# One part's distance between the steps of a split, maxima two outputs later, low halves one product later

## The chip, the cores and the metric

The kernel runs on one core of a Trainium2 chip. The metric is device time of one execution in microseconds; the time before is the median of three runs.

## The reference

Attention over 4 x 8 heads of 576 tokens with a threshold on the scores, then two layers without a residual:

```
x = attention(q, k, v, tau)                # 2304 tokens x 512
a, b = x @ w1, x @ w2                      # 2304 x 1024
x2 = ((a * b) @ w3) @ w_out                # 2304 x 512
h = x2 @ w_in                              # 2304 x 2048
g = where(h > 0, h, exp(min(h, 0)) - 1)
out = g @ w_out2                           # 2304 x 512
```

All inputs are float32. The kernel works with pairs of a high and a low half (two float32r or two float16 tensors whose sum is the number), and every product is three matmuls: high with high, high with low, low with high.

## The kernel before

The attention and the products a and b come first, ordered by a planner; that part ends near 510 us and the change does not touch it. From there on each engine's queue is the order of the Python calls, written by hand. SyncE (SP) issues nearly all DMAs, in order, and a DMA that must wait holds those behind it. POOL below is GpSimd.

**The x2 stage.** w3 and w_out were multiplied into M. The tokens are six blocks of 384 (loop `for x, j in enumerate(JS)`), and each block has four outputs of 128 rows (`e`), each of 24 matmuls into one of four PSUM buffers (`ps_x`). A block's g stands as high and low halves in four slots that all six blocks share: while the last output of a block runs, ScalarE makes the high halves of the next block (line 325) and VectorE the low ones (line 326), and then g of the block after that is loaded. For each output `x_size` (line 1200) takes VectorE's maximum from PSUM, and ScalarE copies the output to SBUF (lines 1351 and 1354; from the third block on through `x2s`, two buffers, to DRAM). Two engines do not read one PSUM buffer at the same time here: the second in the order of the calls waits for the first. Beside that, `run_jobs` converts w_in (lines 336 to 350, maximum in line 1265), forms Strassen-like sums of its quarters on POOL (line 1249) and stores seven parts per pair of hidden tiles to DRAM (line 1241).

**The scales.** The halves are float16, so everything is scaled by powers of two from maxima over a whole tensor. `everywhere` sends a maximum per partition to DRAM (line 988) and reads it back to all partitions (line 991); the function that it returns reduces that on VectorE (line 994). There are four such round trips: x2's first pair of blocks (`xg[:, 0:1]`), the weights (`r2`, which gives `w_to`), the other blocks of x2 (`xg[:, 1:3]`), and the output weights (`o_two`, which gives `shift`). The code sends at one place and calls `seen` at a later one.

**The last stage.** For each of three pairs of blocks (`p`) a step goes over one of eight pairs of hidden tiles (`f`), 24 steps. h of a step is a Strassen-like product: seven products of six matmuls (`product`, line 1459, two PSUM buffers), each with its own combination of x2 blocks (`bs[k]`, made by `high_b` on ScalarE and `low_b` on VectorE) and its own part of w_in (`WI[f][:, k]`). The first product is copied by ScalarE (line 1500), the others are added up by VectorE (`sum_of`, line 1485) into four quarters of h. Each quarter then goes through `elu_low`: a minimum (VectorE, line 1397), its exponential (ScalarE, 1398), the maximum that gives g (VectorE, 1401), the high half (ScalarE, 1403) and the low half (VectorE, 1404). After each product, `after(k)` issues five matmuls of the product with w_out2 for the quarters of the step before (`fill`, line 1418, six PSUM buffers `po`); after the last product it issues what is left of them.

In the first pass over f (p = 0) the parts of w_in are still to be split: `load_u` loads part n to a ring of eight buffers `units`, and `split_u` scales it (POOL, line 1300), takes the high half (ScalarE, 1302) and the low half (POOL, 1303), all in one call. `after` makes up to two such calls. The first four steps also convert the last parts of w_out2 (lines 336 to 350, 1021, 1031 to 1033), and at the end of the fifth step the outputs so far, six PSUM buffers, are multiplied by `shift` (lines 1555 and 1557).

Of the kernel before, what the change touches and what calls it, by code (L numbers as in the profile page):

```python
# [10 lines left out]
F16 = mybir.dt.float16  # L11
I32 = mybir.dt.int32
U16 = mybir.dt.uint16
AF = mybir.ActivationFunctionType
ALU = mybir.AluOpType
# [4 lines left out]
P = 128  # L20
# [12 lines left out]
TB = 384  # L33
NB = NT // TB
NPR = NB // 2
NH = NF2 // 2
NC = 7
NUR, NUS = (4, 4), (4, 3)
LEAST_X, LEAST = 2.0 ** -45, 2.0 ** -30
NPL = 4  # L40
WARM = 6
# [227 lines left out]
def attention_moe_moe2(  # L269
# [14 lines left out]
    V, A, G, T, SP = nc.vector, nc.scalar, nc.gpsimd, nc.tensor, nc.sync  # L284
# [10 lines left out]
    W = [None] * 8  # L295
# [518 lines left out]
    for p in range(NPL, NPAIR):  # L814
        t0 = AT[p, 0]
        firsts = [i for i in range(NTILE) if SEQ[i][0] == p]
        for j in range(2):
            h = 2 * p + j
# [259 lines left out]
    def run_jobs(k):  # L1078
        for _ in range(k):
            if jobs:  # L1080
                for fn in jobs.pop(0):
                    fn()
# [116 lines left out]
    def x_size(x, e, o):  # L1199
        V.tensor_reduce(xm[:, 4 * x + e:4 * x + e + 1], o, axis=AX.X, op=ALU.max, apply_absolute_value=True)  # L1200
# [84 lines left out]
    def load_u():  # L1285
        if nu[0] < len(USEQ):
# [2 lines left out]
            SP.dma_start(units[nu[0] % sum(NUR)], wi_dr[f, k])  # L1289
            nu[0] += 1  # L1290

    def split_u():
        n = ns[0]
        if n < len(USEQ):
            f, k = USEQ[n]
            if f not in WI:
                pool, tag = (wp, f"W{4 + f}") if f < 4 else (hop, f"WI{f}")
                WI[f] = pool.tile([P, NC, 2, 2, P], F16, tag=tag, name=f"WI{f}", bufs=1)
            r, t = units[n % sum(NUR)], WI[f][:, k]
            G.tensor_scalar(r, r, w_to, 0.0, op0=ALU.mult, op1=ALU.add)  # L1300
            r = r.rearrange("p (k c) -> p k c", k=2)
            A.activation(t[:, 0], r, AF.Copy)  # L1302
            G.tensor_tensor(t[:, 1], r, t[:, 0], op=ALU.subtract)  # L1303
            ns[0] += 1

    for x, j in enumerate(JS):
        half = x % 2
        for e in range(NK):
# [14 lines left out]
            if x == NB - 1 and e == NK - 1:  # L1323
                for k in (3, 4):
                    high_b(k, 0)
                    low_b(k, 0)
            x_size(x, e, o[:, :TB])
            if x == 2 and e == 0:
                x_sizes(0, xg[:, 0:1])
                seen = everywhere(xg[:, 0:1])  # L1330
            if x == 2 and e == 2:
                seen(xg[:, 0:1])
                x_scale((0,))
            if x == NB - 1 and e == 0:
# [2 lines left out]
                    r2[:, 1:2], cols("wo_two", 8).rearrange("p (a b) -> p a b", a=2)[:, :, :2], axis=AX.XY, op=ALU.max  # L1337
                )
                seen = everywhere(r2)
            if x == NB - 1 and e == 1:  # L1340
                seen(r2)
                power(w_two, r2[:, 0:1], LEAST, 1.0)
                V.tensor_scalar(w_to, w_two, 2.0 ** -11, None, op0=ALU.mult)
                V.reciprocal(w_to, w_to)
                V.tensor_copy(o_two[:, 0:1], r2[:, 1:2])
                h_scale((0,), o_two[:, 0:1])
# [20 lines left out]
            for _ in range(1 + (x * NK + e in (0, 2))):  # L1367
                if len(jobs) > LATE:
                    run_jobs(1)
    run_jobs(len(jobs) - LATE)  # L1370
    ps2.close()
    xw.close()
    mp.close()
# [17 lines left out]
    def elu_low(c):  # L1391

        x, name, dst = c["x"], c["name"], c["dst"]

        def one():
            t = c["t"] = tmp("et", f"et{name}", 2)
            V.tensor_scalar(t, x, 0.0, None, op0=ALU.min)  # L1397
            A.activation(t, t, AF.Exp)  # L1398

        def two():  # L1400
            V.scalar_tensor_tensor(x, c["t"], -1.0, x, op0=ALU.add, op1=ALU.max)  # L1401
            h = hop.tile([P, 2, TB], F16, tag="gg", name=f"gg{name}", bufs=8)
            A.activation(h[:, 0, :], x, AF.Copy, scale=c["by"])  # L1403
            V.scalar_tensor_tensor(h[:, 1, :], x, c["by"], h[:, 0, :], op0=ALU.mult, op1=ALU.subtract)  # L1404
            dst["h"] = h

        return one, two

    def o_mms(p, f, half, dst, first, last):

# [31 lines left out]
            except StopIteration:  # L1442
                oq.pop(0)

    late, highb = [], []
    steps = [(p, f) for p in range(NPR) for f in range(NH)]
    for s, (p, f) in enumerate(steps):
        nm = f"{p}_{f}"
# [4 lines left out]
        def product(k):  # L1453
            w = WI[f][:, k]
            o = ps_h.tile([P, 512], F32, tag="h", name=f"h{nm}_{k}")
            i = 0
            for kt in range(2):
                for wx, xx in ((0, 0), (0, 1), (1, 0)):
                    T.matmul(  # L1459
                        o[:, :TB], w[:, wx, kt, :], bs[k][:, kt, xx, :],  # L1460
                        start=(i == 0), stop=(i == 5),
                    )
                    i += 1
            return o[:, :TB]
# [29 lines left out]
        def plus(n, a, b):  # L1494
            return sum_of(thin[n], a, b)
# [16 lines left out]
        after(0)  # L1512

        u2 = plus(1, product(1), m1)
        after(1)

        quarter("11", product(2), m1)
# [22 lines left out]
        quarter("21", product(5), u3)  # L1540
        lows["22"][1]()
        lows["21"][0]()
        after(5)

        quarter("12", product(6), u4)
        lows["21"][1]()
        lows["12"][0]()
        late.append(lows["12"][1])
        after(6, 99)
        if s == NH // 2:  # L1550
            for h in range(2):
                for t in range(TB // P):
                    o = po[JS[h], t]
                    if t % 2:
                        V.tensor_scalar(o, o, shift, None, op0=ALU.mult)
                    else:
                        A.activation(o, o, AF.Copy, scale=shift)  # L1557
        for q in ("11", "22", "21", "12"):
            oq.append(o_mms(p, f + (NH if q[0] == "2" else 0), int(q[1]) - 1, gg[q], f == 0 and q in ("11", "22"),
                            f == NH - 1 and q in ("21", "12")))  # L1560
        if p + 1 < NPR and f == 1:
            for h in range(2):
                SP.dma_start(bq[:, h], x2_dr[JS[2 * p + 2 + h]])
    while late:
        late.pop(0)()
    fill(999)


# [45 lines left out]
```

## Time and profile before

| | |
|---|---|
| time, median of three runs | 1071.73 us (1071.66 to 1072.56) |
| profiled execution | 1074.29 us, span 1072.5 us |
| granted TensorE clock, mean | 0.969 |
| TensorE busy | 966.8 us (90% of the span) |
| VectorE busy | 771.0 us (72%) |
| ScalarE busy | 556.0 us (52%) |
| GpSimd busy | 437.6 us (41%) |

Times inside the trace count from the start of the span. The granted clock is a share of TensorE's upper level, 2.4 GHz; at the lower one, 1.2 GHz, it is 0.5. Matmuls are pipelined and their ends are modelled, so a TensorE that is shown as busy may still be slow. An idle time in square brackets stands before an instruction, with what ended it.

### The profile page before, as it was taken

The numbers are of one execution on the slowest core, as the hardware profiler recorded it, in microseconds if no ns is written. First come the engines' busy times: TensorE is split into PE (matmuls) and PEld (weight loads), VectorE is DVE, ScalarE is ACT, GpSimd is POOL, SyncE is SP. The second block draws the span as 40 slices with busy tenths as digits, with TensorE's granted clock in tenths as the row PEclk, the third lists the DMA queues.
The fourth block names the chain that finished last, engine by engine and source line by source line (L and its number), as shares of the span: only waits on it lengthen the run. The fifth ranks groups of instructions, "written<-read, shape, count | busy, mean of one in ns | idle before, by whom it ended". The sixth has DMA issues, their size and how long they took to land. (4 is left out here: it accounts for less than half of the span.)

```text
span 1072.5 us, 17102 instructions
## 1 busy us (share of the span) xinstructions
PE 966.8 (90%) x6074; PEld 698.5 (65%) x6074; DVE 771.0 (72%) x1448; ACT 556.0 (52%) x945; POOL 437.6 (41%) x608
## 2 busy tenths in 40 slices
PE   7899999999999999989998876786898999989998
PEld 4456887788889899977897862333344544445553
DVE  6888886888777884979775645665567666766665
ACT  5777776876766763445333424443454333443333
POOL 3468775878788972534210235554340000000000
PEclk9999999999999999999998997988899999999999
DMA  8436765667899787756476564411100200010001
GB/s 250 146 123 157 167 164 133 174 183 182 163 197 192 176 170 221 251 210 241 140 243 213 204 208 124 142 40 47 40 11 29 89 1 1 1 60 1 1 1 60
DMA packets 167282, 138.18 MB, mean 129 GB/s; under 512 B 118332, under 2 KB 153884, under 8 KB 162588
## 3 DMA queue, kind: packets, MB, share of 16 engines
q1 hardware_dynamic: 163084, 107.43, 37.5%
q10 hardware_dynamic: 4112, 29.66, 7.9%
q8 instruction: 48, 0.79, 0.3%
q14 instruction: 38, 0.31, 0.1%
HBM read 84.61 MB, written 24.72 MB: 102 GB/s over the span
## 5 line engine op out<-in xcount | busy, mean ns | idle before, releaser
L1459 PE MATMUL h<-so,WI 128*128 128x384 f16 x1008 | 201.9, 340 | 54.5 <-DVE th L1485 31.4
L681 PE MATMUL ab<-x,W 128*128 128x256 f32 (+1 forms) x1536 | 223.8, 298 | 5.9 <-DVE g L696 4.6
L1418 PE MATMUL o<-WO,gg 128*128 128x512 f16 x864 | 220.7, 390 | 5.8 <-ACT o L1557 4.9
L681 PEld LDWEIGHTS ab<-x,W 128*128 128x128 f32 x1536 | 207.5, 188 | 15.0 <-issue 5.7
L1459 PEld LDWEIGHTS <-WI 128*128 128x128 f16 x1008 | 101.3, 101 | 151.6 <-issue 70.7
L1418 PEld LDWEIGHTS <-gg 128*128 128x128 f16 x864 | 86.3, 100 | 96.3 <-issue 14.4
L526 DVE SCALAR_TENSOR_TENSOR e<-s,st,e 128x576 f32<-128x576 f32 x144 | 115.2, 808 | 23.9 <-ACT e L520 21.8
L1485 DVE SCALAR_TENSOR_TENSOR th<-h,back,th 128x384 f32<-128x384 f32 x168 | 99.0, 611 | 41.5 <-PE h L1459 37.8
L1398 ACT ACTIVATE et<-et 128x384 f32<-128x384 f32 x96 | 50.2, 523 | 143.3 <-DVE et L1397 142.2
L1404 DVE SCALAR_TENSOR_TENSOR gg<-th,c_by,gg 128x384 f16<-128x384 f32 x96 | 60.5, 630 | 87.7 <-ACT gg L1403 87.7
L537 POOL TENSOR_TENSOR hl<-e,hl 128x512 f16<-128x512 f32 x94 | 110.8, 1179 | 25.1 <-ACT hl L533 18.9
L502 DVE TENSOR_REDUCE st<-s 128x1 f32<-128x576 f32 x144 | 105.9, 749 | 18.1 <-PE s L492 10.1
L1313 PE MATMUL x<-sl,M 128*128 128x384 f32 x576 | 107.8, 350 | 10.5 <-DVE sl L326 6.3
L1313 PEld LDWEIGHTS x<-sl,M 128*128 128x128 f32 x576 | 105.2, 198 | 13.0 <-DVE sl L326 8.1
L1403 ACT ACTIVATE gg<-th,c_by 128x384 f16<-128x384 f32 x96 | 58.8, 613 | 71.2 <-DVE th L1401 71.2
L520 ACT ACTIVATE e<-s,st 128x576 f32<-128x576 f32 x108 | 78.4, 736 | 25.6 <-POOL st L510 16.7
L492 PE MATMUL s<-qk 128*128 128x288 f32 x480 | 83.2, 306 | 5.6 <-DVE e L526 4.7
L492 PEld LDWEIGHTS s<-qk 128*128 128x128 f32 x480 | 68.0, 189 | 14.3 <-issue 7.7
L533 ACT ACTIVATE hl<-e 128x576 f16<-128x576 f32 x94 | 63.1, 681 | 22.8 <-DMA pt<-hl 11.2
L1303 POOL TENSOR_TENSOR WI<-wr,WI 128x256 f16<-128x256 f32 x56 | 43.5, 777 | 67.1 <-ACT WI L1302 67.1
L1401 DVE SCALAR_TENSOR_TENSOR th<-et,th 128x384 f32<-128x384 f32 x96 | 54.4, 566 | 17.4 <-ACT et L1398 13.1
L480 PE MATMUL s<-qkp 128*64 128x288 f32 x288 | 43.1, 435 | 7.2 <-ACT pt L578 3.7
(137 smaller groups left out, 1359.2 us busy)
## 6 DMA issues: line engine op xcount, KB each, us to landing
rqk<-in_qk SPq DMA_DIRECT2D x24, 576.0 KB
raw_wo<-in_wo ACTq DMA_DIRECT2D x12, 1024.0 KB
th<-g_dr SPq DMA_DIRECT2D x48, 192.0 KB
raw_w<-in_w SPq DMA_DIRECT2D x8, 1024.0 KB
raw_w<-in_w3t ACTq DMA_DIRECT2D x8, 1024.0 KB
raw_win<-in_win ACTq DMA_DIRECT2D x8, 1024.0 KB
wr<-wi_dr SPq DMA_DIRECT2D x56, 128.0 KB
vr<-in_v SPq DMA_DIRECT2D x16, 320.0 KB
```

The source lines that it names most:

```text
L492: T.matmul(s[:, n, :HS], q, k[:, c:c + HS], start=(x == 0), stop=(x == len(ops) - 1))
L502: V.tensor_reduce(st[i][:, 0:1], sc[i][:, :, :HS], axis=AX.XY, op=ALU.max if plain else ALU.min, negate=plain)
L520: A.activation(et[i], sc[i][:, :, :HS], AF.Exp, bias=st[i][:, k:k + 1], scale=esc if plain else -1.0)
L526: V.scalar_tensor_tensor(et[i], sc[i][:, :, :HS], st[i][:, 1:2], et[i], op0=ALU.is_ge if p < NPL else ALU.is_le, op1=ALU.mult, accum_out=s ...
L533: A.activation(hl[i][:, :S], et[i].rearrange("p a b -> p (a b)"), AF.Copy)
L537: G.tensor_tensor(t[:, S + 64:], e[:, :512], t[:, :512], op=ALU.subtract)
L681: T.matmul(o[:, :w], wf[:, m, wx, kt, :], x[:, xx, :], start=(kt == 0 and k == 0), stop=(kt == NK - 1 and k == 2),)
L1313: T.matmul(o[:, :TB], M[:, f, mx, e * P:(e + 1) * P], gh[j, f][:, gx, :], start=(k == 0), stop=(k == 23),)
L1404: V.scalar_tensor_tensor(h[:, 1, :], x, c["by"], h[:, 0, :], op0=ALU.mult, op1=ALU.subtract)
L1418: T.matmul(po[j, t], dst["h"][:, gx, t * P:(t + 1) * P], WO[f // 2 % 4][:, f // 8, f % 2, wx, :], start=(first and k == 0), stop=(stop and ...
L1459: T.matmul(o[:, :TB], w[:, wx, kt, :], bs[k][:, kt, xx, :], start=(i == 0), stop=(i == 5),)
L1485: V.scalar_tensor_tensor(x, a, back[:, p:p + 1], b, op0=ALU.mult, op1=ALU.add)
```

## The change

- `split_u`: a call now scales part n, takes the high half of part n - 1 and the low half of part n - 2. Two more calls run ahead (`NUS` from (4, 3) to (6, 3), so three calls instead of two at each of the last two outputs of x2), and all eight loading buffers exist from the x2 stage on and are loaded there at once (`NUR` from (4, 4) to (8, 0)).
- `x_size` of an output is issued after the matmuls of the output two later, so behind ScalarE's copy of its own output. The maximum of x2's first pair is sent two outputs later (block 2, output 2 instead of 0) and read two outputs later (block 3, output 0); the maximum of the weights is sent at the same place and read one output later (block 5, output 2).
- `elu_low` has a third part: the low half of g (line 1404) is issued one product after the high half. For the last two quarters of a step that is in the next step (lists `late` and `later`).
- The multiplication of the outputs by `shift` in the fifth step is in two halves: the first block's three after product 5, the second's after product 6.

```diff
-NUR, NUS = (4, 4), (4, 3)
+NUR, NUS = (8, 0), (6, 3)
@@ split_u
         n = ns[0]
         if n < len(USEQ):
-            ...
-            r, t = units[n % sum(NUR)], WI[f][:, k]
+            r = units[n % sum(NUR)]
             G.tensor_scalar(r, r, w_to, 0.0, op0=ALU.mult, op1=ALU.add)
-            r = r.rearrange("p (k c) -> p k c", k=2)
+        if 0 < n <= len(USEQ):
+            r, t = half_of(n - 1)
             A.activation(t[:, 0], r, AF.Copy)
+        if 1 < n <= len(USEQ) + 1:
+            r, t = half_of(n - 2)
             G.tensor_tensor(t[:, 1], r, t[:, 0], op=ALU.subtract)
-            ns[0] += 1
+        ns[0] += 1
@@ x2 stage
-            x_size(x, e, o[:, :TB])
-            if x == 2 and e == 0:
+            unsized.append((x, e, o[:, :TB]))
+            while len(unsized) > 2:
+                x_size(*unsized.pop(0))
+            if x == 2 and e == 2:
                 x_sizes(0, xg[:, 0:1])
                 seen = everywhere(xg[:, 0:1])
-            if x == 2 and e == 2:
+            if x == 3 and e == 0:
                 seen(xg[:, 0:1])
                 x_scale((0,))
...
-            if x == NB - 1 and e == 1:
+            if x == NB - 1 and e == 2:
                 seen(r2)
@@ elu_low
-            V.scalar_tensor_tensor(h[:, 1, :], x, c["by"], h[:, 0, :], op0=ALU.mult, op1=ALU.subtract)
-            dst["h"] = h
-        return one, two
+            dst["h"] = h
+        def three():
+            h = dst["h"]
+            V.scalar_tensor_tensor(h[:, 1, :], x, c["by"], h[:, 0, :], op0=ALU.mult, op1=ALU.subtract)
+        return one, two, three
@@ the steps
         u2 = plus(1, product(1), m1)
+        while later:
+            later.pop(0)()
...
         lows["21"][0]()
+        lows["11"][2]()
         after(5)
+        if s == NH // 2:
+            rescale(0)
...
         lows["12"][0]()
-        late.append(lows["12"][1])
+        lows["22"][2]()
+        late += [lows["12"][1], lows["21"][2]]
+        later.append(lows["12"][2])
         after(6, 99)
         if s == NH // 2:
-            for h in range(2):
-                ...
+            rescale(1)
```

## Rows read from the trace of the kernel before

**Rows 1.** Table of windows: length, busy us (instructions) per engine, granted clock, DMA share, GB/s.
```profile
514.02:632.29 118.27, 107.78 (x577) 105.03 (x575) 76.12 (x113) 40.83 (x76) 25.38 (x17) 0.94 0.58 190
644.36:668.49 24.13, 15.25 (x50) 6.74 (x50) 13.91 (x27) 10.61 (x22) 13.88 (x18) 0.71 0.47 133
668.49:736.88 68.39, 51.13 (x235) 24.52 (x234) 44.63 (x87) 31.23 (x59) 36.76 (x45) 0.90 0.22 72
736.88:813.65 76.77, 64.26 (x315) 31.84 (x314) 51.34 (x104) 34.61 (x70) 26.97 (x45) 0.93 0.11 33
846.11:861.27 15.16, 14.76 (x79) 7.61 (x78) 9.56 (x19) 5.02 (x11) 0.00 (x0) 1.00 0.01 2
861.27:877.08 15.81, 14.97 (x79) 7.61 (x78) 11.13 (x21) 5.02 (x11) 0.00 (x0) 1.00 0.00 1
923.20:940.61 17.41, 15.12 (x79) 7.60 (x78) 14.35 (x25) 9.98 (x17) 0.00 (x0) 1.00 0.00 1
940.61:957.90 17.29, 15.24 (x78) 7.60 (x78) 12.57 (x24) 7.94 (x15) 0.00 (x0) 1.00 0.12 45
```
**Rows 2.** Timeline of TensorE in the x2 stage: start, us, instruction, count, idle before.
```profile
514.02 16.98 PE L1313 MATMUL x<-sl,M 128*128 128x384 f32 x97
...
573.05 0.44 PE L1313 MATMUL x<-sl,M 128*128 128x384 f32 x1 [3.81 <-ACT sl L325]
574.87 19.22 PE L1313 MATMUL x<-sl,M 128*128 128x384 f32 x95 [1.38 <-DVE sl L326]
...
597.36 34.93 PE L1313 MATMUL x<-sl,M 128*128 128x384 f32 x191 [2.44 <-DVE sl L326]
...
644.97 4.83 PE L1459 MATMUL h<-so,WI 128*128 128x384 f16 x18 [6.12 <-ACT th L1500]
```
**Rows 3.** Timeline of VectorE, eight low halves at two block boundaries.
```profile
530.44 7.23 DVE L326 TENSOR_TENSOR sl<-th,sl 128x384 fp32r<-128x384 f32 x8
...
574.26 3.83 DVE L326 TENSOR_TENSOR sl<-th,sl 128x384 fp32r<-128x384 f32 x8
```
**Rows 4.** Groups of instructions, 514 to 640 us: busy, mean ns, idle before and why.
```profile
L1354 ACT ACTIVATE x2s<-x 128x384 f32<-128x384 f32 x15 | 7.4, 491 | 54.4 <-DVE xm L1200 34.3 <-issue 9.3 <-DVE x_two L980 8.6
```
**Rows 5.** Timeline at two round trips, SyncE, VectorE and TensorE.
```profile
559.75 0.32 SPq L988 DMA_DIRECT2D mx_dr<-xg  x1
...
570.56 0.28 DVE L994 TENSOR_REDUCE xg<-mxb 128x1 f32<-128x128 f32 x1 [4.89 <-DMA mxb<-mx_dr]
...
726.12 0.32 SPq L988 DMA_DIRECT2D mx_dr<-o_two  x1
...
738.57 0.27 DVE L994 TENSOR_REDUCE o_two<-mxb 128x1 f32<-128x128 f32 x1
...
743.36 1.37 PE L1459 MATMUL h<-so,WI 128*128 128x384 f16 x6 [3.54 <-DVE th L1485]
```
**Rows 6.** Waits in the first pass, 644.36 to 813.65: us in total, times, longest.
```profile
DVE gg L1404 <- ACT gg L1403: 40.8, 31, 5.2
...
ACT WI L1302 <- POOL wr L1300: 38.3, 25, 2.7
```
**Rows 7.** Timeline around the end of the third step.
```profile
705.97 2.12 POOL L1033 TENSOR_TENSOR WO<-w_wo,WO 128x1024 f16<-128x1024 f32 x1 [3.87 <-ACT WO L1032]
...
709.53 0.63 DVE L1404 SCALAR_TENSOR_TENSOR gg<-th,c_by,gg 128x384 f16<-128x384 f32 x1 [5.18 <-ACT gg L1403]
...
711.01 2.08 PE L1459 MATMUL h<-so,WI 128*128 128x384 f16 x6 [4.76 <-DVE th L1485]
```
**Rows 8.** Timeline where two plain later steps meet.
```profile
971.66 0.62 DVE L1404 SCALAR_TENSOR_TENSOR gg<-th,c_by,gg 128x384 f16<-128x384 f32 x1 [0.68 <-ACT gg L1403]
...
972.20 0.35 DVE L1397 TENSOR_SCALAR et<-th 128x384 f32<-128x384 f32 x1
...
973.07 0.56 ACT L1500 ACTIVATE th<-h,back 128x384 f32<-128x384 f32 x1
...
973.69 1.14 PE L1459 MATMUL h<-so,WI 128*128 128x384 f16 x6 [0.40 <-ACT th L1500]
```

More of the change, by code (lines that the diff above doesn't have):

```diff
@@ L1290, in load_u, with half_of @@
             nu[0] += 1
+    def half_of(n):
+        f, k = USEQ[n]
+        if f not in WI:
+            pool, tag = (wp, f"W{4 + f}") if f < 4 else (hop, f"WI{f}")
+            WI[f] = pool.tile([P, NC, 2, 2, P], F16, tag=tag, name=f"WI{f}", bufs=1)
+        return units[n % sum(NUR)].rearrange("p (k c) -> p k c", k=2), WI[f][:, k]
     def split_u():
@@ L1294, in split_u @@
         if n < len(USEQ):
[L1295 to L1298, printed above, removed]
-            r, t = units[n % sum(NUR)], WI[f][:, k]
+            r = units[n % sum(NUR)]
             G.tensor_scalar(r, r, w_to, 0.0, op0=ALU.mult, op1=ALU.add)
-            r = r.rearrange("p (k c) -> p k c", k=2)
+        if 0 < n <= len(USEQ):
+            r, t = half_of(n - 1)
             A.activation(t[:, 0], r, AF.Copy)
+        if 1 < n <= len(USEQ) + 1:
+            r, t = half_of(n - 2)
             G.tensor_tensor(t[:, 1], r, t[:, 0], op=ALU.subtract)
-            ns[0] += 1
+        ns[0] += 1
+    unsized = []
     for x, j in enumerate(JS):
@@ L1370, in attention_moe_moe2 @@
     run_jobs(len(jobs) - LATE)
+    while unsized:
+        x_size(*unsized.pop(0))
     ps2.close()
@@ L1443, in fill, with rescale @@
                 oq.pop(0)
-    late, highb = [], []
+    def rescale(h):
+        for t in range(TB // P):
+            o = po[JS[h], t]
+            if t % 2:
+                V.tensor_scalar(o, o, shift, None, op0=ALU.mult)
+            else:
+                A.activation(o, o, AF.Copy, scale=shift)
+    late, later, highb = [], [], []
     steps = [(p, f) for p in range(NPR) for f in range(NH)]
@@ L1547, in attention_moe_moe2 @@
         lows["12"][0]()
-        late.append(lows["12"][1])
+        lows["22"][2]()
+        late += [lows["12"][1], lows["21"][2]]
+        later.append(lows["12"][2])
         after(6, 99)
         if s == NH // 2:
-            for h in range(2):
[L1552 to L1557, printed above, removed]
+            rescale(1)
         for q in ("11", "22", "21", "12"):
@@ L1563, in attention_moe_moe2 @@
                 SP.dma_start(bq[:, h], x2_dr[JS[2 * p + 2 + h]])
-    while late:
-        late.pop(0)()
+    for fn in late + later:
+        fn()
     fill(999)
```

## The prediction

> **What bounds the kernel now.** I first cut the span into its stages with the table of windows. Up to 514 us the change touches nothing. The x2 stage (514.02 to 632.29), the first pass over the hidden quarters (eight steps, 644.36 to 813.65) and two further passes of eight steps each are left. The reader is to compare each window's length with what TensorE needs. A plain later step is 15.16 us at full clock with VectorE 9.6 us busy; the steps of the first pass last 20 to 24 us at a granted clock of 0.71 to 0.93 of the 2.4 GHz level, and no engine in them is busy throughout [rows 1]. So the first pass is bound by waiting. The TensorE timeline then shows where: in the x2 stage 97 products run in 16.98 us (0.173 us each, 4.15 us for an output of 24), so 24 outputs need 99.5 us of the 118.3, and 18.8 us are lost at block boundaries, with one more hole before 644.97 [rows 2]. The waits of the first pass name a ring: ScalarE waits 38.3 us for GpSimd's scaling in split_u, and VectorE waits 40.8 us for ScalarE's high half of g [rows 6]. One turn of it stands in the timeline: GpSimd's subtraction for WO ends at 708.09, its next scaling follows, VectorE stands 5.18 us before a low half, and TensorE 4.76 us behind VectorE; the six products after it take 2.08 us where a step at full clock has 1.14 [rows 7, 8].
>
> **The change part by part.** The sum is made against the profiled execution, 1074.29 us (span 1072.5); the median of the runs, 1071.73, lies 2.6 lower.
>
> *Maxima two products late (x2 stage).* Nothing is added; 24 reductions move. Today ScalarE's copy of an output is issued behind VectorE's maximum of it, and waits 34.3 us for it in all [rows 4]; afterwards it needs TensorE alone, and the maximum finds its copy long made. PSUM has four buffers for x2, so a maximum two outputs late still frees one in time. Three boundaries pay today. After the first block the eight low halves take 7.23 us instead of 3.83, beside GpSimd's sums [rows 3]; VectorE will come there up to 2 us sooner, and I take 3 us of gain. Before the fourth block TensorE idles 3.81 + 1.38 us, and 95 products then take 19.22 us instead of 16.4 [rows 2]: 8 us, because VectorE sits in the round trip of the largest maximum (559.75 to 570.56, 10.8 us [rows 5]) and the copies' stores queue behind it on SyncE. The reading moves a block later and the round trip goes behind two copies' stores and the seven stores of w_in's parts on SyncE; I take 7 of the 8. The price is at the next boundary (2.44 us idle today, about 4.8 with the slow products behind it [rows 2]): the answer now lands near 576, VectorE makes scales and low halves of b after that, and comes to its subtractions no earlier against TensorE than today. I take 0.5 of gain there, between a loss of 3 and a gain of 4.8. Sum 10.5, bounds 4 to 16.
>
> *Start of the first pass.* TensorE's two first h products end and it stands 6.12 us [rows 2], because ScalarE serves four splits in turn with GpSimd, a copy behind its maximum, and four high halves before it may copy product 0. With scaling, high part and low part one call apart, none of these waits for an engine that has just been asked. Back to back they are some 6.5 us of ScalarE after the weights' scale is known (about 632.6), so product 0 is copied near 639.7 instead of 644.9. The eight unit loads issued at once cost SyncE some 2.7 us more in front of one store; x2s buffers hide that. Gain 5, bounds 2 to 8.
>
> *Splits one part apart, low half of g one product later (first pass).* No instruction is added; 56 calls of split_u lose the hand-over inside a call. The number of finished parts ahead of TensorE stays: two more calls ahead, two in flight. Step 0: 24.13 us with VectorE and GpSimd each 13.9 busy [rows 1]; bounds 14 and 24, I take 18.5, near the middle since every output of it hangs on a VectorE chain. Steps 1 to 3: 68.39 us, with VectorE 14.9 and GpSimd 12.3 busy per step, TensorE 14.6 at full clock [rows 1, 8]. Bounds 14.9 and 22.8 a step. I take 16.5, nearer the lower end because the idle that fills the rest is the ring that the edit cuts, and 2 us more for step 1, where VectorE will come to the second round trip before it has landed: 51.5, a gain of 16.9.
>
> Steps 4 to 7 are 76.77 us [rows 1]. Half of the rescaling of o goes one product forward; today all six stand together and hold TensorE 4.9 us, and this goes. But step 4 gets a new wait. The largest output scale is sent off at 726.12 in step 3 and read at 738.57 without a wait; 4.8 us of small operations later TensorE goes on [rows 5]. That round trip is about 10.8 long by the row at 559.75. In a step 3 of 16.5 us it starts 10.5 in, lands 5 us into step 4, and TensorE resumes 9.8 us into that step, where it could at 5: a stall of 5, and 2.8 more for slow products afterwards as after the 4.76 us stall. So step 4 is 22.4, steps 5 to 7 are 14.8, 14.7 and 15.4: 67.3, a gain of 9.5.
>
> *Low half of g in the later passes.* At a step's end VectorE waits 0.68 us before a low half at 971.66; behind it stand the next minimum (972.20), its exponential, and ScalarE's copy of product 0 (973.07), for which TensorE waits [rows 8]. With the low half behind the minimum that chain moves 1.2 us forward; TensorE's stall is about 0.6 (15.16 against 14.55 of its own). So 11 plain steps gain 0.6 each (6.6), the two of 15.81 with the sums of b 0.9 each (1.8), the one of 17.41 about 1.8 (VectorE is 14.35 busy there, so it may bound at 15.6), the two of 17.29 about 2.3 each [rows 1]. Sum 14.8, bounds 4 and 18. What is late next is TensorE itself.
>
> Sum: 10.5 + 5 + 5.6 + 16.9 + 9.5 + 14.8 = 62.3. 1074.3 less 62.3 is 1012, and 1009.5 as a median of runs.
>
> *A rule against it.* The row first: the same eight VectorE subtractions take 7.23 us beside GpSimd's sums and 3.83 without them [rows 3]. The Trainium skill, "SBUF — State Buffer", section "Who interferes with whom", says why: a VectorE instruction with two SBUF inputs and a GpSimd instruction that reads SBUF hold one pair of ports exclusively, and the loser blocks. The trace agrees (0.90 against 0.48 us each).
>
> **The rivals.**
> 1. *The two engines block each other.* Waits removed put GpSimd's 12.3 us of a step beside VectorE's 14.9 more often, and stretch it as in rows 3. If a third of GpSimd's time is added to VectorE's, steps 0 to 3 stay near 19 to 19.5 and steps 4 to 7 lose 2: the first pass gives back 11, and the time is 1021. For it: rows 3. Against it: the reductions, minima and sums that read PSUM, about half of VectorE's work here, take one tensor from SBUF or none. By the skill's rule it is this case that comes out.
> 2. *The steady step keeps its stall*, because something else than the low half delays the copy of product 0: the later passes give 2 instead of 14.8, 1022. Against: the chain of rows 8 has no other link.
> 3. *The new round-trip waits are hidden* (VectorE later than I think, or the answer sooner) and steps reach 15: gain 75, 997.
> 4. *Slower: the round trips.* All four readings of a maximum stand where VectorE has less to do before them. Each holds TensorE for its length less some 6 us that two h buffers and queued work cover, plus 2.8 of slow products. The rest of the change is worth 62 + 8 (the stall that I charged to step 4) = 70 us, so it decides from a round trip of about 21 us at all four; the rows have 10.8 and at most 12.5 [rows 5]. SyncE's longer queue in front of them speaks for it. At 22 us the time is 1075.
> 5. *Nothing moves*: the order of issue is not what the code says. Against: VectorE's and ScalarE's order in the rows follows the code. 1072.
>
> **How the numbers follow.** Chances: forecast 0.46 (its own range 1000 to 1018), rival 1 0.20, rival 2 0.12, rival 3 0.14, rival 4 0.04, rival 5 0.02; 0.02 for rivals 1 and 2 together (1034). I predict 1009.5. Rivals 1 and 2 set the upper end, with their sizes uncertain: 1036. The lower end, with every step at 15 and all boundaries gone, is 985. What a measurement can tell from no change is 0.2%, 2 us: faster 0.94, same 0.02, slower 0.04.
>
> **What would show it.** ScalarE's waits for the maxima gone in the x2 stage; no idle before the fourth block, some before the fifth. ScalarE's wait for GpSimd's scaling and VectorE's for the high half of g each down by more than half. Step 4 the longest, behind VectorE waiting for a DMA; plain later steps at 14.5 to 14.6 us. I am wrong if steps 1 to 3 stay over 20 us, if plain steps stay at 15.16, or if a new DMA wait stands in front of every stage.

## The result, and the profile after

The changed kernel takes 1026.64 us (median of four runs, 1024.54 to 1027.93), the kernel before 1071.7; the ratio is 0.9581, with a 95% interval of 0.9559 to 0.9604. The forecast was 1009.5 in a range of 985 to 1036: faster, as forecast, and 17 us less so. The profiled execution took 1027.93 us with a span of 1026.1, so the spans differ by 46.4 us where the sum of the prediction had 62.3.

The table of windows of the kernel after, cut as in [rows 1]: the x2 stage, step 0, steps 1 to 3, steps 4 to 7, and a plain later step. Columns are the window, its length, busy us (instructions) of TensorE, its weight loads, VectorE, ScalarE and GpSimd, the granted clock, the DMA share and GB/s.
```profile
513.01:629.81 116.80, 105.75 (x577) 103.56 (x575) 76.62 (x117) 41.53 (x77) 25.83 (x18) 0.94 0.59 194
636.49:658.39 21.90, 13.52 (x52) 6.29 (x52) 15.37 (x28) 10.17 (x22) 12.20 (x17) 0.69 0.65 203
658.39:717.73 59.34, 46.90 (x234) 23.28 (x234) 51.23 (x87) 30.58 (x58) 40.10 (x46) 0.97 0.28 91
717.73:783.79 66.06, 59.01 (x308) 30.46 (x308) 53.00 (x104) 32.75 (x68) 29.14 (x45) 0.97 0.12 36
840.36:854.96 14.60, 14.60 (x80) 7.64 (x78) 10.90 (x21) 4.69 (x11) 0.00 (x0) 1.00 0.00 1
```
Set beside [rows 1], each line is one term of the prediction:

| stage | before | after | gain | forecast |
|---|---|---|---|---|
| ahead of the x2 stage | 514.02 | 513.01 | 1.0 | 0 |
| x2 stage | 118.27 | 116.80 | 1.5 | 10.5 |
| its end to the copy of product 0 | 12.07 | 6.68 | 5.4 | 5 |
| step 0 | 24.13 | 21.90 | 2.2 | 5.6 |
| steps 1 to 3 | 68.39 | 59.34 | 9.1 | 16.9 |
| steps 4 to 7 | 76.77 | 66.06 | 10.7 | 9.5 |
| the two later passes | 258.8 | 242.3 | 16.5 | 14.8 |

Three terms are short: the x2 stage by 9.0 us, steps 1 to 3 by 7.8, step 0 by 3.4. The others together are 4.3 better than forecast. Differences of a microsecond in the first rows say little: the x2 stage begins between 511.1 and 515.6 us in the runs below, and takes 116.8 to 118.4 us in those that leave its maxima and buffers as they are after the change. In steps 1 to 3 VectorE's busy time rose from 44.63 to 51.23 us for the same 87 instructions: that is the number to remember.

**The x2 stage.** TensorE's timeline of the kernel after (start, us, instruction, count, idle before and its releaser):
```profile
513.01 62.84 PE L1321 MATMUL x<-sl,M 128*128 128x384 f32 x360
579.69 5.76 PE L1321 MATMUL x<-sl,M 128*128 128x384 f32 x24 [3.83 <-DVE xm L1200]
589.87 0.66 PE L1321 MATMUL x<-sl,M 128*128 128x384 f32 x1 [4.42 <-ACT sl L325]
593.12 1.33 PE L1321 MATMUL x<-sl,M 128*128 128x384 f32 x3 [2.58 <-DVE sl L326]
```
Against [rows 2], the holes before the second and the fourth block have gone: 360 products run without one. They come back a little later, as 3.83 us behind a maximum (line 1200) and 4.42 + 2.58 us at the fifth block. The timelines of SyncE, ScalarE and VectorE around the first hole, with ScalarE's next copy behind it:
```profile
560.98 0.68 SPq L988 DMA_DIRECT2D mx_dr<-xg  x1
571.11 0.33 SPq L991 DMA_DIRECT2D mxb<-mx_dr  x1
571.53 0.38 SPq L1365 DMA_DIRECT2D x_dr<-x2s  x1
...
576.18 0.49 ACT L1364 ACTIVATE x2s<-x 128x384 f32<-128x384 f32 x1 [11.69 <-PE x L1321]
...
583.73 0.49 ACT L1364 ACTIVATE x2s<-x 128x384 f32<-128x384 f32 x1 [5.22 <-DMA x_dr<-x2s]
...
574.23 0.28 DVE L994 TENSOR_REDUCE xg<-mxb 128x1 f32<-128x128 f32 x1 [2.87 <-DMA mxb<-mx_dr]
...
577.53 1.02 DVE L1189 SCALAR_TENSOR_TENSOR so<-bq,x_to,so 128x768 f16<-128x768 f32 x1 [2.26 <-ACT so L1185]
...
579.09 0.54 DVE L1200 TENSOR_REDUCE xm<-x 128x1 f32<-128x384 f32 x1
```
The load of the answer (line 991) holds SyncE until the store of the maximum has landed, 10.1 us after its issue. The store of a copy `x2s` stands behind it, and behind that eight loads of g. ScalarE makes its next copy only at 576.18. The profile names TensorE for that wait, but the output was ready more than 8 us sooner (312 products at 0.175 us from 513.01 on); right in front of the copy on ScalarE's queue stands a load of w_in (575.75), which by the trace's semaphores had waited for the landing of the first of those loads of g. The high half of b is behind the copy, VectorE's low half (577.53) behind the high half, and the maximum that frees TensorE's PSUM buffer (579.09) behind the low half. For the copy at 583.73 it is the buffer: there are two `x2s`, and it waits for the landing of a store. The high halves of g for the fifth block come after it, and the holes of 4.42 and 2.58 us stand at the start of that block.

**The first pass.** Waits from 636.49 to 783.79 (us in total, times, longest), against [rows 6]:
```profile
ACT WI L1307 <- POOL wr L1304: 22.5, 12, 6.1
...
DVE th L1413 <- ACT et L1410: 10.4, 12, 1.5
...
DVE o_two L994 <- DMA mxb<-mx_dr: 2.9, 1, 2.9
```
VectorE's 40.8 us of waiting for ScalarE's high half of g have no row any more; ScalarE's 38.3 for GpSimd's scaling have become 22.5, which is not the "more than half" that the prediction gave as a sign. What VectorE now does longer is seen in two groups of it, in steps 1 to 3 and then from 855 to 1000, where GpSimd does nothing (busy, mean ns):
```profile
L1413 DVE SCALAR_TENSOR_TENSOR th<-et,th 128x384 f32<-128x384 f32 x13 | 11.5, 888 | 8.6 <-ACT et L1410 8.6
L1420 DVE SCALAR_TENSOR_TENSOR gg<-th,c_by,gg 128x384 f16<-128x384 f32 x12 | 9.3, 773 | 0.0
...
L1420 DVE SCALAR_TENSOR_TENSOR gg<-th,c_by,gg 128x384 f16<-128x384 f32 x40 | 24.4, 611 | 0.0
L1413 DVE SCALAR_TENSOR_TENSOR th<-et,th 128x384 f32<-128x384 f32 x40 | 22.1, 552 | 2.6 <-ACT et L1410 2.4
```
The thirteenth of the maxima in the first row begins at 658.04, still in step 0. Beside these two groups, the conversions for w_out2 in steps 1 to 3 (lines 343, 347 and 350) take 10.8 us instead of 8.2, while the 21 sums that read PSUM stay at 0.61 us each. One of the long maxima in the timelines of VectorE and GpSimd:
```profile
714.10 1.36 DVE L1413 SCALAR_TENSOR_TENSOR th<-et,th 128x384 f32<-128x384 f32 x1 [1.04 <-ACT et L1410]
...
712.91 2.12 POOL L1033 TENSOR_TENSOR WO<-w_wo,WO 128x1024 f16<-128x1024 f32 x1 [5.45 <-ACT WO L1032]
```
The maximum that gives g starts while GpSimd subtracts for w_out2 (its low half). GpSimd ends at 715.03, the maximum 0.43 us later. Of the twelve maxima in steps 1 to 3, six overlap with GpSimd and take 1.20 us on average, six don't and take 0.55. In the kernel before, nine of twelve overlap with GpSimd as well, and none is longer than 0.56. The timelines of VectorE and GpSimd there show the difference:
```profile
701.03 0.54 DVE L1401 SCALAR_TENSOR_TENSOR th<-et,th 128x384 f32<-128x384 f32 x1
...
701.07 1.03 POOL L1303 TENSOR_TENSOR WI<-wr,WI 128x256 f16<-128x256 f32 x1 [1.22 <-ACT WI L1302]
```
Here the maximum comes 0.04 us ahead, and it is GpSimd's subtraction that takes 1.03 us instead of 0.67. So it is in all nine: GpSimd begins up to 0.36 us later, and its subtraction takes 0.73 to 1.10. Once it is shown 0.02 us sooner and is the one that gets longer all the same, so a lead that small does not tell who was first. The Trainium skill, "SBUF — State Buffer", section "Who interferes with whom", has for this "Issue order, not op shape, decides who blocks", and the trace agrees: GpSimd's 2.12 us stand as in [rows 7] where it was first, and VectorE waits it out. After the change GpSimd is first, by 0.04 to 1.18 us, at these six maxima. So the maxima do not meet GpSimd more often than before, they meet it in the other order.

**Step 4.** The timelines of SyncE, VectorE and TensorE:
```profile
709.89 0.32 SPq L988 DMA_DIRECT2D mx_dr<-o_two  x1
716.93 0.32 SPq L991 DMA_DIRECT2D mxb<-mx_dr  x1
...
722.06 0.28 DVE L994 TENSOR_REDUCE o_two<-mxb 128x1 f32<-128x128 f32 x1 [2.89 <-DMA mxb<-mx_dr]
...
726.70 2.08 PE L1482 MATMUL h<-so,WI 128*128 128x384 f16 x6 [6.14 <-DVE th L1508]
```
The forecast put a new stall here, of 5 us in a step of 22.4; it is 6.14 in a step of 22.65. 7.04 us of the round trip are a store of 4 bytes per partition on its way.

### The profile page after: what moved, and what is told of

Same layout as the page of the kernel before. It is cut to its first block, busy times and chain, and to the rows that moved or that the text cites. A ratio compares the mean times of both kernels' runs of the same rounds, so it can differ in the third digit from the quotient of the medians.

```text
span 1026.1 us, 17137 instructions
## 1 busy us (share of the span) xinstructions
PE 948.0 (92%) x6074; PEld 693.3 (68%) x6074; DVE 778.3 (76%) x1448; ACT 549.3 (54%) x945; POOL 444.2 (43%) x608
## 5 line engine op out<-in xcount | busy, mean ns | idle before, releaser
L1482 PE MATMUL h<-so,WI 128*128 128x384 f16 x1008 | 196.6, 333 | 32.1 <-DVE th L1508 18.6
L1433 PE MATMUL o<-WO,gg 128*128 128x512 f16 x864 | 214.3, 381 | 0.0
L526 DVE SCALAR_TENSOR_TENSOR e<-s,st,e 128x576 f32<-128x576 f32 x144 | 115.2, 808 | 24.1 <-ACT e L520 22.4
L537 POOL TENSOR_TENSOR hl<-e,hl 128x512 f16<-128x512 f32 x94 | 110.8, 1179 | 24.9 <-ACT hl L533 18.4
L502 DVE TENSOR_REDUCE st<-s 128x1 f32<-128x576 f32 x144 | 106.0, 750 | 17.5 <-PE s L492 10.1
L1321 PE MATMUL x<-sl,M 128*128 128x384 f32 x576 | 105.7, 346 | 11.1 <-ACT sl L325 4.4
L1413 DVE SCALAR_TENSOR_TENSOR th<-et,th 128x384 f32<-128x384 f32 x96 | 59.4, 618 | 14.8 <-ACT et L1410 14.2
L1420 DVE SCALAR_TENSOR_TENSOR gg<-th,c_by,gg 128x384 f16<-128x384 f32 x96 | 62.9, 655 | 0.2 <-ACT gg L1415 0.2
```

Of the source, the lines that this page charges most:

```text
L502: V.tensor_reduce(st[i][:, 0:1], sc[i][:, :, :HS], axis=AX.XY, op=ALU.max if plain else ALU.min, negate=plain)
L526: V.scalar_tensor_tensor(et[i], sc[i][:, :, :HS], st[i][:, 1:2], et[i], op0=ALU.is_ge if p < NPL else ALU.is_le, op1=ALU.mult, accum_out=s ...
L537: G.tensor_tensor(t[:, S + 64:], e[:, :512], t[:, :512], op=ALU.subtract)
L1321: T.matmul(o[:, :TB], M[:, f, mx, e * P:(e + 1) * P], gh[j, f][:, gx, :], start=(k == 0), stop=(k == 23),)
L1433: T.matmul(po[j, t], dst["h"][:, gx, t * P:(t + 1) * P], WO[f // 2 % 4][:, f // 8, f % 2, wx, :], start=(first and k == 0), stop=(stop and ...
L1482: T.matmul(o[:, :TB], w[:, wx, kt, :], bs[k][:, kt, xx, :], start=(i == 0), stop=(i == 5),)
```

## The experiments

Ratios are against the kernel before on the same chip (medians of 1075 to 1077 us there). The first three put one part each into the kernel before.

**Splits alone.** `split_u`, `NUR` and `NUS` as after the change, all else as before:
```
-NUR, NUS = (4, 4), (4, 3)
+NUR, NUS = (8, 0), (6, 3)
...
+            r, t = half_of(n - 1)
             A.activation(t[:, 0], r, AF.Copy)
+            r, t = half_of(n - 2)
             G.tensor_tensor(t[:, 1], r, t[:, 0], op=ALU.subtract)
...
```


> The kernel before with the splits one part apart and nothing else. Theory (the ring ScalarE-GpSimd set the first pass, and VectorE's waits for the high half of g hung on it): ScalarE's wait for GpSimd's scaling falls from 38 us to under 20, the start gains some 4 us, the first pass some 12, the later passes nothing: 1054, 1048 to 1060. Rival (VectorE's wait before the low half of g is the first pass's own limit, the ring only rides along): only the start gains, 1066 or more.

1070.5 us, ratio 0.9958 (0.9939 to 0.9976). The window of steps 1 to 3:
```profile
666.11:732.69 66.58, 50.04 (x237) 24.02 (x235) 50.62 (x87) 30.91 (x58) 41.82 (x46) 0.93 0.24 77
```
ScalarE's wait for GpSimd's scaling falls from 28.9 to 5.5 us in steps 0 to 3, so the hand-over inside a call went. Yet steps 1 to 3 are only 1.8 us shorter than before, the start 1.8 and step 0 3.0; VectorE is 6 us longer busy in steps 1 to 3 and GpSimd 5. That the stretch took what the hand-over gave fits this, but is not shown by itself. VectorE still waits for the high half of g (16.3 us in steps 0 to 3, 28.3 before). The rival holds.

**Maxima alone.**
```
-            x_size(x, e, o[:, :TB])
-            if x == 2 and e == 0:
+            unsized.append((x, e, o[:, :TB]))
+            while len(unsized) > 2:
+                x_size(*unsized.pop(0))
+            if x == 2 and e == 2:
...
```


> The kernel before with the maxima of x2 two outputs late and their round trips moved, and nothing else. Theory (the stall before the fourth block only moves to the fourth and fifth, since the reading of the first maximum and SyncE's queue behind it block as long as before): the x2 stage keeps 115 to 118 us, the time is 1068 to 1072. Rival (the stage's loss in the changed kernel comes from the splits or the loading buffers, not from the moved maxima): the stage falls to some 108 us, the time to 1062.

1072.38 us, ratio 0.9972 (0.9956 to 0.9989). TensorE's timeline in the x2 stage:
```profile
581.57 6.01 PE L1314 MATMUL x<-sl,M 128*128 128x384 f32 x24 [3.50 <-DVE xm L1200]
591.90 0.66 PE L1314 MATMUL x<-sl,M 128*128 128x384 f32 x1 [4.33 <-ACT sl L325]
595.15 1.33 PE L1314 MATMUL x<-sl,M 128*128 128x384 f32 x3 [2.58 <-DVE sl L326]
```
The same three stalls as in the kernel after, with the same releasers, so this part makes them by itself: it moves the stall. The stage is 116.5 us long, as the theory had it. Product 0 is copied 3.9 us sooner after it than before, and step 0 is 3.8 us longer.

**Low half alone.**
```
+        def three():
+            h = dst["h"]
             V.scalar_tensor_tensor(h[:, 1, :], x, c["by"], h[:, 0, :], op0=ALU.mult, op1=ALU.subtract)
...
```


> The kernel before with the low half of g one product later and nothing else. Theory: the sixteen later steps give 16 us as in the changed kernel, a plain one is 14.6 us; the first pass gives 5 to 10 since VectorE no longer stands behind ScalarE: 1048, 1042 to 1056. Rival (the later steps owe their gain to something else): plain steps stay at 15.16 and the time over 1062.

1040.33 us, ratio 0.9690 (0.9667 to 0.9714), the larger part of the gain. The window of steps 1 to 3 and that of step 0:
```profile
667.16:727.87 60.71, 49.26 (x234) 24.03 (x234) 47.59 (x87) 31.53 (x58) 38.53 (x45) 0.92 0.25 81
645.01:667.16 22.15, 13.43 (x52) 6.01 (x52) 14.52 (x28) 10.50 (x22) 14.20 (x18) 0.80 0.50 143
```
The steps are as short as after the whole change to within 1.4 us, and VectorE's busy time has already grown by 3 us. The two later passes take 242.4 us and a plain step 14.6, as the theory had it: all of their gain comes from this part. The first pass gives 18.2 us where the theory had 5 to 10, and the time lies below its range.

**The first maximum on GpSimd's queue.** In the kernel after, the store and load of x2's first maximum are issued by GpSimd instead of SyncE:
```
-                seen = everywhere(xg[:, 0:1])
+                seen = everywhere(xg[:, 0:1], G)
```


> The changed kernel, with the DMAs of the first round trip (store and reading back of x2's first maximum) issued by GpSimd instead of SyncE. Theory (SyncE stands before the reading until the store has landed, and behind it x2's copies, and ScalarE, and VectorE's maxima, and TensorE's PSUM): the idle times of TensorE of 3.8 us inside the fourth block and 7 us before the fifth go or fall by two thirds, the x2 stage is 105 to 109 us instead of 116.8, the time 1016 to 1019. Rival (the late maxima themselves hold PSUM and VectorE, whoever issues the DMAs): the stage stays over 114 and the time at 1025 or more.

1026.29 us, ratio 0.9550 (0.9528 to 0.9572), not to be told from the kernel after. TensorE, VectorE and GpSimd:
```profile
573.45 19.15 PE L1321 MATMUL x<-sl,M 128*128 128x384 f32 x96 [7.50 <-DVE sl L326]
...
572.21 0.75 DVE L343 TENSOR_SCALAR w_win<-raw_win 128x1024 uint16<-128x1024 uint16 x1 [10.05 <-DMA wi_dr<-s]
...
572.81 0.57 POOL L991 DMA_DIRECT2D mxb<-mx_dr  x1 [10.79 <-DMA wi_dr<-s]
```
SyncE does not wait for the landing now, and the stage is still 114.6 us: one hole of 7.50 us and two small ones stand where three were. VectorE's conversion and GpSimd's load of the answer both start after 572, and the profile names a store of w_in's parts for both. The load also needs the maximum's own store, which GpSimd issued at 561.29, so that name need not be the right one there. The theory's 105 to 109 us are not met; time and stage are those of the rival, but the rows do not show its late maxima as the cause. What held all of them until 572 is open (last section).

**Eight bytes.** In the kernel after, the two maxima of one column travel as two, the second without use:
```
+    xp2 = cols("xp2", 2)
+    V.memset(xp2, 0.0)
...
-                x_sizes(0, xg[:, 0:1])
-                seen = everywhere(xg[:, 0:1])
+                x_sizes(0, xp2[:, 1:2])
+                seen = everywhere(xp2)
...
-            seen = everywhere(o_two[:, 1:2])
+            seen = everywhere(o_two)
```


> The kernel after the change, but the two maxima of one column (x2's first pair and the output weights) are sent as two columns, 8 bytes per partition instead of 4, the other column without use. Theory: the landing time of such a store hangs on the 4 bytes (7.0 us from 709.89 to 716.93 after the change) against 3 us for 8 bytes (650.74 to 653.63); so both round trips are some 4 us shorter, TensorE's 6.14 us before 726.70 in step 4 falls to about 2, the 3.83 us in the x2 stage goes or moves, and the time is 1016 to 1021. Rival: the landing time has to do with what else the queue holds at these places; then the two stores still take 6 us or more and the time stays at 1026.

1020.39 us, ratio 0.9487 (0.9440 to 0.9534). SyncE at both round trips, then ScalarE and TensorE in the x2 stage:
```profile
560.95 0.66 SPq L988 DMA_DIRECT2D mx_dr<-xp  x1
564.98 0.33 SPq L991 DMA_DIRECT2D mxb<-mx_dr  x1
...
705.76 0.32 SPq L988 DMA_DIRECT2D mx_dr<-o_two  x1
709.04 0.32 SPq L991 DMA_DIRECT2D mxb<-mx_dr  x1
...
579.73 0.49 ACT L1367 ACTIVATE x2s<-x 128x384 f32<-128x384 f32 x1 [5.66 <-DMA x_dr<-x2s]
...
585.87 0.66 PE L1324 MATMUL x<-sl,M 128*128 128x384 f32 x1 [6.11 <-ACT sl L325]
```
The theory holds: 4.0 us instead of 10.1 at the first place and 3.3 instead of 7.0 at the second. Step 4 falls from 22.65 to 18.58 us. TensorE's 6.14 us there become 1.45. In the x2 stage 3.1 us go, and 6.11 stay at the fifth block, behind a copy that waits for a buffer `x2s`.

**Four buffers x2s**, on top of that:
```
-                t = xwp.tile([P, TB], F32, tag="x2s", name=f"x2s{j}_{e}", bufs=2)
+                t = xwp.tile([P, TB], F32, tag="x2s", name=f"x2s{j}_{e}", bufs=4)
```


> The kernel of eight_byte_maxima with four buffers x2s instead of two for the copies of x2. Theory: what is left in the x2 stage (TensorE 6.11 us before the fifth block, 585.87 in eight_byte_maxima) is ScalarE waiting 5.66 us for a buffer x2s, whose store stands behind eight loads of g on SyncE, and the high halves of g behind that copy; with four buffers ScalarE's wait goes, the 6.11 us falls below 3, and the time is 1015 to 1018. Rival: VectorE's low halves beside GpSimd's sums (2.60 us before the next output, 589.13) are late as well and take its place; the stage keeps its length and the time is 1020.

1015.16 us, ratio 0.9420 (0.9399 to 0.9441). TensorE's timeline:
```profile
514.59 68.55 PE L1324 MATMUL x<-sl,M 128*128 128x384 f32 x385
586.00 1.33 PE L1324 MATMUL x<-sl,M 128*128 128x384 f32 x3 [2.87 <-DVE sl L326]
```
The theory holds. The x2 stage is 108.4 us, 9.9 less than in the kernel before: the 10.5 of the prediction were there, behind a 4-byte store and two buffers. What is left, 2.87 us, is VectorE's low half. Four buffers with the 4-byte store were not run.

**Late read in step 4.** In the kernel after, the output weights' answer is read behind the third product of step 4, not ahead of the first:
```
-        if s == NH // 2:
-            seen(o_two[:, 1:2])
...
         lows["11"][0]()
+        if s == NH // 2:
+            seen(o_two[:, 1:2])
```


> The kernel after the change, but the answer of the output weights' maximum is read behind the third product of step 4, not ahead of its first. Theory: TensorE's 6.14 us in step 4 is VectorE waiting for that answer with the step's first minima queued behind it; read later, it has landed, and step 4 takes 16 to 17 us instead of 22.65: 1019 to 1021. Rival: the weights' halves that follow from the answer are then late for what comes next, and the stall moves to step 5 with its length: 1025.

1022.61 us, ratio 0.9503 (0.9458 to 0.9549). The store still lands after 7.45 us, but step 4 takes 17.83 us and step 5 the 13.28 that it had. The theory holds, with 4.8 us of the step; step and time end a little above its 16 to 17 and 1019 to 1021.

**Scaling on ScalarE**, in the kernel after:
```
-            G.tensor_scalar(r, r, w_to, 0.0, op0=ALU.mult, op1=ALU.add)
-            r, t = half_of(n - 1)
+            A.activation(r, r, AF.Copy, scale=w_to)
             A.activation(t[:, 0], r, AF.Copy)
```


> The kernel after the change, but ScalarE and not GpSimd multiplies each part of w_in by its scale (in a call of its own with the high half behind it); GpSimd only subtracts. Theory: VectorE and GpSimd stretch each other in steps 1 to 3 (VectorE 51.2 us busy in the window after the change, 44.6 before); with GpSimd's 8 us of scaling gone from these steps, VectorE's busy time falls to about 47, its maxima from 888 ns to about 650, and steps 1 to 3 take 53 to 56 us instead of 59.3: 1019 to 1023. Rival: the first pass is bound by the chain through ScalarE, which gets 0.4 us more per part; then VectorE gets shorter and the steps don't, 1026 or more.

1025.38 us, ratio 0.9537 (0.9482 to 0.9591), not to be told from the kernel after. Its windows: steps 1 to 3, step 0, step 4.
```profile
655.00:711.90 56.90, 47.75 (x234) 23.47 (x234) 50.04 (x87) 40.70 (x79) 25.15 (x25) 0.94 0.31 97
637.28:655.00 17.72, 12.28 (x52) 5.73 (x52) 14.04 (x27) 14.53 (x31) 8.41 (x8) 0.84 0.61 207
...
711.90:736.22 24.32, 16.72 (x78) 8.05 (x78) 17.42 (x43) 12.68 (x28) 7.32 (x10) 0.86 0.19 63
```
Steps 0 to 3 lose 6.6 us and step 4 takes 1.7 of them back. The start takes 1.8 us more (8.50 for 6.68). The theory got the size of VectorE wrong: 15 us of GpSimd's work less shorten it by 1.2 us only, not 4, and steps 1 to 3 and the time miss its ranges. So the amount of GpSimd's work alone does not set the stretch.

**No wait for GpSimd**, in the kernel after: ScalarE scales within its high half, GpSimd scales just ahead of its subtraction.
```
-            A.activation(t[:, 0], r, AF.Copy)
+            A.activation(t[:, 0], r, AF.Copy, scale=w_to)
...
+            G.tensor_scalar(r, r, w_to, 0.0, op0=ALU.mult, op1=ALU.add)
             G.tensor_tensor(t[:, 1], r, t[:, 0], op=ALU.subtract)
```


> The kernel after the change, but ScalarE takes the high half with the scale in its own instruction from the unscaled part, so that it waits for no scaling by GpSimd; GpSimd scales two calls later, just ahead of its subtraction. GpSimd's work is the same as before. Theory (hand-over): ScalarE's 22.5 us of waits for the scaled part in the first pass are what holds it; they go, and the time falls to 1016 to 1020. Rival (ports): GpSimd's and VectorE's instructions stretch each other as now, VectorE's busy time in steps 1 to 3 stays near 51 us, and the time is 1024 to 1027.

1027.01 us, ratio 0.9537 (0.9493 to 0.9582), again no difference. Steps 1 to 3 and step 4:
```profile
659.02:713.81 54.79, 45.38 (x234) 22.84 (x234) 49.03 (x87) 31.64 (x59) 42.63 (x46) 1.00 0.30 99
...
713.81:739.19 25.38, 16.91 (x76) 8.21 (x76) 16.77 (x43) 9.64 (x21) 14.82 (x23) 0.80 0.19 55
```
By its time the port rival holds, by its rows the hand-over: steps 1 to 3 are 4.6 us shorter with no less work on GpSimd. Step 4 is 2.7 us longer: the maximum is sent 6.8 us ahead of it instead of 7.8, its store takes 7.53 us, and it is read 6.1 us into the step instead of 4.3.

**All together**, twice: four buffers, 8 bytes, the late read, and one of the last two edits each.

> The kernel of four_x2s_buffers with the late read of late_read_step4 and ScalarE's high half without a wait of no_wait_for_gpsimd. Theory: no_wait_for_gpsimd shortened steps 1 to 3 from 59.3 to 54.8 us, and the read in step 4 took it back (25.4 us instead of 22.65), because the landing of that maximum does not come sooner with shorter steps. With the wait for the landing out of the way both gains stay: steps 1 to 3 at 55, step 4 at 17 to 18, and 5 us below four_x2s_buffers. Rival: something else than the landing takes it back in steps 4 to 7 (the parts of w_in or their halves arrive late); then within 1.5 us of four_x2s_buffers.

> The kernel of four_x2s_buffers with the late read of late_read_step4 and ScalarE's scaling of scaling_on_scalar. Theory (ports): GpSimd's scaling beside VectorE costs steps 0 to 3 some 6.6 us (81.2 to 74.6 in scaling_on_scalar), and only step 4 took it back; steps 0 to 3 at 74 to 75, step 4 at 17 to 18, 6 to 7 us below four_x2s_buffers. Rival: as for all_and_no_wait; within 1.5 us of four_x2s_buffers.

1011.21 us, ratio 0.9392 (0.9376 to 0.9408), and 1010.36, ratio 0.9378 (0.9364 to 0.9392): some 1.5 to 2% below the kernel after. Against four_x2s_buffers they gain 4 and 5 us. So for both the theory's direction holds: with the landing out of the way, the gains of steps 1 to 3 stay. Step 4 is 18.4 and 19.2 us, a little over the 17 to 18 expected. The windows of steps 1 to 3, first one and then the other:
```profile
647.32:702.12 54.80, 45.39 (x234) 22.84 (x234) 49.03 (x87) 31.64 (x59) 42.63 (x46) 1.00 0.34 102
```
```profile
648.01:704.43 56.42, 46.80 (x234) 23.22 (x234) 49.80 (x87) 40.69 (x79) 24.52 (x25) 0.97 0.34 101
```

**No split on GpSimd**, from the first of these two:
```
-            A.activation(t[:, 0], r, AF.Copy, scale=w_to)
...
-            G.tensor_scalar(r, r, w_to, 0.0, op0=ALU.mult, op1=ALU.add)
-            G.tensor_tensor(t[:, 1], r, t[:, 0], op=ALU.subtract)
+            r = units[n % sum(NUR)].rearrange("p (o c) -> p o c", o=1)
+            A.activation(t.rearrange("p g k c -> p g (k c)"), r.to_broadcast([P, 2, 256]), AF.Copy, scale=w_to)
```


> The kernel of all_and_no_wait without GpSimd's scaling and subtraction of w_in's parts: ScalarE writes its high half into the place of the low half as well, in the same instruction (the low halves of w_in are left out of the computation). GpSimd is left with its sums for w_out2 alone. Theory (ports): in the kernel after the change the maximum that gives g takes 1.20 us beside GpSimd and 0.55 without it, and what is missing in steps 1 to 3 against the forecast is this stretch. VectorE's busy time in these steps falls from 49 us to 45 or 46, and the steps from 54.8 to 51 or 52, the 51.5 of the forecast; the first step loses its 5.6 us stall too: 1003 to 1006. Rival (the chain of minimum, exponential and maximum through ScalarE): VectorE gets shorter and waits longer for ScalarE, steps 1 to 3 stay at 54 to 55, 1010.

1004.15 us, ratio 0.9356 (0.9326 to 0.9387). Steps 1 to 3, and then VectorE's group of the maximum there:
```profile
648.40:699.24 50.84, 44.90 (x234) 22.84 (x234) 43.56 (x88) 35.84 (x59) 6.39 (x3) 1.00 0.35 111
```
```profile
L1411 DVE SCALAR_TENSOR_TENSOR th<-et,th 128x384 f32<-128x384 f32 x13 | 8.7, 671 | 6.6 <-ACT et L1408 6.6
```
This run leaves the low halves of w_in out, to see the time alone. The port theory holds: GpSimd's splits gone, VectorE is at 43.56 us, below the kernel before, and the steps at 50.84. VectorE's wait for the exponential grows by 1.2 us only (5.4 in all_and_no_wait), so the rival's chain is there but doesn't bind. Step 0 falls from 22.50 to 19.36.

## Why the prediction was right in sign and 17 us short

**Later passes, start, step 4: right in size, with some luck.** Plain steps are 14.60 us with TensorE never idle (forecast 14.5 to 14.6), so rival 2 is out; the later passes give 16.5 where 14.8 stood, and low_half_alone gives the same. The start gives 5.4 for 5, but not by the part that the prediction had behind it: splits_alone has 1.8 us of it, and maxima_alone 3.9, which its step 0 takes back. Step 4's new stall is 6.14 for 5, so rival 3 is out, and eight_byte_maxima and late_read_step4 each take some 4 to 5 us of the step away by its supposed cause. Its size is luck in part: the round trip is 12.2 us instead of the 10.8 assumed, but step 3 is 19.7 instead of 16.5, so more of the trip fell into step 3 (7.8 us for some 6). Steps 4 to 7 give 10.7 for 9.5.

**The x2 stage: 10.5 forecast, 1.5 measured. The term that failed** is "I take 0.5 of gain there, between a loss of 3 and a gain of 4.8", and in part the "I take 7 of the 8" ahead of it. By the timelines of [rows 2] and of the kernel after, the fourth block's last product ended 80.07 us after the start of the stage and now ends after 72.44: 7.6 us of gain where the first two terms had 10. From there to the end of the stage it was 38.20 us and is 44.36: a loss of 6.2, outside the bounds of the third term. (The smaller slip beside it: 16.98 us for 97 products are 0.175 us each, not 0.173, some 1 us over the stage.) The prediction saw that the round trip would go behind more stores, and that its answer would land near 576 (it was read at 574.23). It followed VectorE from there and no other queue. SyncE's waiting load stands in front of the loads of g and of the store that frees a buffer `x2s`, and so ScalarE's copies, its high halves of b, VectorE's low halves and a maximum all stood behind the landing. Maxima_alone shows that this part makes the stall, eight_byte_maxima and four_x2s_buffers that the store's landing and the two buffers hold it: with both eased, the stage gains 9.9 us.

**Steps 1 to 3: 16.9 forecast, 9.1 measured. The term that was mis-sized** is VectorE's 14.9 us a step: it became 17.1. The prediction had 51.5 us for these steps, 44.6 of work and 6.9 of idle. Measured are 51.2 of work and 8.1 of idle, so the idle that it kept was nearly right, and 6.6 of the 7.8 us that are missing are the stretch. That is the mechanism of rival 1, which put these steps near 19 to 19.5 each (19.8 measured, with step 1's 20.85). The prediction itself held that its "rule against it" speaks for this rival, and gave it 0.20. It held "against" it that half of VectorE's work reads PSUM. That half did stay as it was (the sums, 0.61 us each), and the traces show that the other half is enough: one maximum goes from 0.55 to 1.20 us where GpSimd is first. The maxima did not meet GpSimd more often, as the rival had it; the order changed.

With GpSimd's splits away, VectorE is at 43.6 and the steps at 50.8, the size that the forecast had. How much of the 8.5 us between that and the kernel after is port and how much hand-over is bounded by one run more: no_wait_for_gpsimd takes off 4.6 with no less work on GpSimd, 2.2 of them VectorE's own busy time; the last 4.0 go only with GpSimd's splits themselves. The prediction weighed the two as alternatives; they are coupled, because cutting the hand-over waits changes what runs beside what. Of the two waits that it called a ring, one was the limit: low_half_alone gives 7.7 of the 9.1 us, splits_alone 1.8, though ScalarE's wait for the scaling all but goes there.

**Step 0: 5.6 forecast, 2.2 measured.** VectorE's timeline in its beginning:
```profile
640.26 0.74 DVE L343 TENSOR_SCALAR w_wo<-raw_wo 128x1024 uint16<-128x1024 uint16 x1 [4.73 <-DMA wi_dr<-w_win]
```
The first conversion for w_out2 waits for the stores of w_in's last parts; before the change it ran at 640.05 without a wait. The step begins 7.9 us sooner, the stores do not. In scaling_on_scalar the same conversion ran at 635.32 without a wait, and the step was 17.72, below the 18.5 forecast. That fits, but ScalarE's scaling differs there too, and its step 0 begins 1.8 us later after the x2 stage. In no_split_on_gpsimd the conversion still waits, 3.68 us, and the step is 19.36, 3.1 less than with the splits on GpSimd: so these cost time here as well. No run took the stores away, and the step varies from 20.64 to 21.90 in five runs with the same code there: the cause of step 0 stays open.

**The other rivals.** Rival 4, slower by the round trips, did not come near: step 4 stalls 6.14 us, x2's first maximum 3.83 and what follows it, and step 1, with the second round trip, is 20.85 against 18.80 and 19.69 for steps 2 and 3. Rival 5 is out by the rows of the waits.

## What to carry to other kernels

When a round trip through DRAM is moved, follow every engine that stands behind the waiting load on its DMA queue, through the loads and the buffers that it holds up, not only the engine that reads the answer. When waits between engines are cut, expect the order to change in which instructions that read two SBUF tensors meet GpSimd's, and put the stretch into the sum from rows of both orders (here 0.55 to 1.20 us for one). A wait that is hidden behind another, as in step 4, has to go first before a gain upstream of it is seen.

## What the runs showed of the hardware that was not expected

A store of 4 bytes per partition (0.5 KB in all) is slow to land: 7.04 us at 709.89 after the change, 7.45 in late_read_step4, 7.06 at 726.12 in the kernel before. The same store with 8 bytes took 3.28 us in eight_byte_maxima, at the same place behind the same kind of loads; at the x2 stage it was 10.1 against 4.0. Why 4 bytes are slow was not tried.

In first_max_by_gpsimd_queue the DMA engines were shown 0.84 busy from 566 to 570 while they moved only 22 GB/s, with a 4-byte store and the stores of w_in's parts in flight together. In the kernel after they were idle from 566 to 571 in the same wait. Whether the 4-byte store held the others up there stays open.
